# Taps in 64x64 tiles and a reordered front part, in a fused long convolution and MLP

## The chip, the cores and the metric

The kernel runs on one core of a Trainium2 chip. The metric is device time of one execution in microseconds (us). The core has five engines that run beside each other: PE (TensorE, with its weight loads, PEld), DVE (VectorE), ACT (ScalarE), POOL (GpSimd) and SP, which only issues DMAs here. Each works through its own queue in order and waits on the others by semaphores.

## The reference

Sequence length S = 2048, width D = 512, hidden width 1376, bf16 in and out. A causal convolution of four taps on k, a product with v, a convolution as long as the sequence (by FFT in the reference), a gate, and an MLP:

```
k_shift = sum over t of k_pad[:, t:t+S, :] * shift_k[:, 3-t]      # 4 taps, causal
kv      = k_shift * v
y       = irfft(rfft(kv padded to 2S) * rfft(ssm_k padded)) [:S]  # along the sequence, per channel
y       = bf16(y) + kv * ssm_D
h       = q + layernorm(q) * y
out     = h + relu(layernorm(h) @ w1) @ w2
```

## The kernel before

The long convolution is done with discrete Fourier transforms as matmuls, split in two factors. The program order within each engine is written out by hand. Its stages:

1. **Setup.** Tables of sines are made: DVE computes phases (`turns2`), ACT takes the sine (`sines2`, L146), POOL negates (`negated`, L224) into `tab`; POOL also builds `ind`, `ident`, `identw`, `f1w`, the tap weights `wdiag` (L209) and the phases of the inverse tables. `kfl` (the filter, one row per channel and 64 tokens) comes by eight DMAs on SP's and ACT's queues. k and v come transposed (channels on partitions) by eight transposing DMAs on SP's queue, alternating, into `kT` and `vT`; then `x0` (the first tokens of q) and `w1`.
2. **Filter, stage 1** (`stage1`, eight calls `s1`): row-tiled matmuls of kfl with `f1hi` and `f1lo` (L311); ACT and DVE each copy one of the two PSUM pairs into `a1k`.
3. **Taps** (`taps`, eight units `tap`): per unit, two channel blocks of eight matmuls, 128x128 diagonal weights on 512 columns of kT (L339); DVE multiplies the sum with vT in place (L342).
4. **Filter, stage 2** (`second_k`, sixteen calls): eight matmuls with `tab` (L352), copied back into a1k by ACT or DVE.
5. **Rows** (`row`, four calls of `to_rows`): PE transposes vT, two bf16 taken as one fp32 word (L289), and DVE copies the words into `xfl` (L290).
6. **Pairs** (`stage1_pairs`, eight calls): stage 1 for xfl, into `a1x` (L326).
7. **Products** (`product`, sixteen calls): stage 2 for a1x in two orders (u2, u1), each multiplied with a1k. DVE takes u2 (L493); u1 goes to POOL through an ACT copy `usb` (L492, L498) or to DVE.
8. **Inverse**: matmuls with `wd` (L518), a DVE transpose (L523), casts by ACT and POOL (`rounded`), last matmuls with `tf` (L550, L560), the gate (L587, L588).
9. **MLP**: first half L630 with relu on ACT (L666), second half L684, end sum on DVE (L690), output DMAs.

The first norm of q's first tokens (`stats`, `norm_rows`) and the centering of w1 (`column_means` on PE, `center` on POOL) lie between 4 and 6. PSUM is four pairs of banks, handed out in turn by `bank2`: two pools of two, so that each fifth request waits for the reader of the first.

Of the kernel before, what the change touches and what calls it, by code (L numbers as in the profile page):

```python
# [9 lines left out]
ALU = mybir.AluOpType  # L10
# [5 lines left out]
P = 128  # L16
# [39 lines left out]
def kernel(  # L56
# [36 lines left out]

    kfl = front.tile([P, 64, 2, 64], BF16, name="kfl")

    def load_rows(eng, rg):
        for d in range(2):
            src = bass.AP(tensor=A_ssm_k.tensor, offset=A_ssm_k.offset + S * (P * rg + 64 * d), ap=[[64, 32], [S, 64], [1, 64]])
            eng.dma_start(out=kfl[32 * rg:32 * rg + 32, :, d, :], in_=src)

    wsh = consts.tile([P, DC, KS], BF16, name="wsh")
    nc.scalar.dma_start(out=wsh[:], in_=A_shift_k.rearrange("(r p) j -> p r j", p=P))
    scratch = rows.tile([P, 4096], I32, tag="r", name="scratch")
    drow = scratch[:, 4064:4096].bitcast(BF16)
    nc.gpsimd.memset(drow, 0.0)
# [4 lines left out]
    vT = front.tile([P, DC, S], BF16, name="vT")  # L110
    CH = 512
    kT = [front.tile([P, DC, CH + 16], BF16, name=f"kT{c}") for c in range(4)]
    nc.vector.memset(kT[0][:, :, 0:16], 0.0)
    for c in range(4):
        if c == 0:
            nc.sync.dma_start_transpose(out=kT[c][:, :, 16:CH + 16], in_=k_d[0:CH, :])
        else:
            nc.sync.dma_start_transpose(out=kT[c][:], in_=k_d[CH * c - 16:CH * c + CH, :])
        nc.sync.dma_start_transpose(out=vT[:, :, CH * c:CH * c + CH], in_=v_d[CH * c:CH * c + CH, :])

    x0 = front.tile([P, 4, D], BF16, name="x0")
    for b, src in enumerate(_tokens(x_d, 0, 4)):
        nc.sync.dma_start(out=x0[32 * b:32 * b + 32].rearrange("p t d -> p (t d)"), in_=src)


    w1 = w1p.tile([P, DC, DFF], BF16, name="w1")
    for i in range(2):
        for d in range(2):
            nc.sync.dma_start(out=w1[64 * i:64 * i + 64, 2 * d:2 * d + 2],
                                in_=B_w1.rearrange("(c i d g) f -> i d g c f", c=2, i=2, d=2)[i, d])  # L130
# [29 lines left out]
    for s in range(0, P, 64):  # L160
        nc.gpsimd.iota(n2i[s:s + 64, :], pattern=[[0, 1]], base=0, channel_multiplier=1)
    r2 = scratch[:, 0:1024].rearrange("p (a b) -> p a b", b=64)
    nc.gpsimd.iota(r2, pattern=[[2, 16], [128, 64]], base=1, channel_multiplier=0)
    ident = consts.tile([P, P], BF16, name="ident")
# [3 lines left out]

    identw = consts.tile([P, P], F32, name="identw")
    nc.gpsimd.memset(identw[:], 0.0)  # L170
    nc.gpsimd.affine_select(out=identw[:], in_=identw[:], compare_op=ALU.not_equal, fill=1.0,
                            base=0, pattern=[[-1, P]], channel_multiplier=1)

    ind = consts.tile([P, P], BF16, name="ind")
    nc.gpsimd.memset(ind[:], 0.0)
    for s in range(0, P, 32):
        nc.gpsimd.affine_select(out=ind[s:s + 32, :], in_=ind[s:s + 32, :], compare_op=ALU.not_equal, fill=1.0,
                                base=0, pattern=[[-1, P]], channel_multiplier=4)

# [11 lines left out]
    load_rows(nc.scalar, 3)  # L191
    f1hi = consts.tile([P, 64], BF16, name="f1hi")
# [10 lines left out]
    nc.gpsimd.memset(f1w[:], 0.0)  # L203
    for rg in range(DC):
        for i, f in enumerate((f1hi, f1lo)):
            nc.gpsimd.tensor_copy(out=f1w[32 * rg:32 * rg + 32, i, rg % 2, :], in_=f[32 * rg:32 * rg + 32, :])
    wdiag = rows.tile([P, DC, KS, P], BF16, name="wdiag")
    for rg in range(DC):
        nc.gpsimd.tensor_tensor(out=wdiag[:, rg, :, :], in0=ident[:].unsqueeze(1).to_broadcast([P, KS, P]),  # L209
                                in1=wsh[:, rg, :].unsqueeze(2).to_broadcast([P, KS, P]), op=ALU.mult)  # L210
    wm = rows.tile([P, 4, 344], F32, name="wm")
    ones = consts.tile([P, P], BF16, name="ones")
    nc.gpsimd.memset(ones[:], 1.0 / D)

    def turns2(i, b):
        ta = scratch[:, 1024 * (b + 1):1024 * (b + 2)].rearrange("p (a b) -> p a b", b=64)
        _turns(ta, r2, n2c[:], 8192, o2[:, i, b:b + 1])
        return ta
# [7 lines left out]

    o2 = consts.tile([P, 2, 2], F32, name="o2")
    for i in range(2):
        for b in range(2):
            nc.vector.tensor_scalar(out=o2[:, i, b:b + 1], in0=n2c[:], scalar1=32.0 * i, scalar2=4096.0 + 2048.0 * b,  # L230
                                    op0=ALU.mult, op1=ALU.add)
    for b in range(2):
        sines2(0, b, turns2(0, b))
    negated(0)
    negated(1)
# [12 lines left out]
    nc.gpsimd.iota(r3[:], pattern=[[1, 64]], base=0, channel_multiplier=0)  # L248
    for i, (top, bottom) in enumerate(((64.0, 96.0), (48.0, 80.0), (32.0, 64.0), (6144.0, 8192.0))):
        nc.gpsimd.memset(ow[0:64, i:i + 1], top)  # L250
        nc.gpsimd.memset(ow[64:128, i:i + 1], bottom)
    for i in range(3):
        nc.gpsimd.tensor_scalar(out=t3[:, i, :], in0=r3[:], scalar1=n2c[:], scalar2=ow[:, i:i + 1], op0=ALU.mult, op1=ALU.add)
    nc.gpsimd.memset(hsc[:], 0.0)
    nc.gpsimd.memset(hbi[:], 0.0)
    nc.gpsimd.tensor_scalar(out=k1o[:], in0=k1c[:], scalar1=2.0, scalar2=1.0, op0=ALU.mult, op1=ALU.add)
    for b in range(4):
        q = slice(32 * b, 32 * b + 32)
        nc.gpsimd.memset(hsc[q, b % 2:b % 2 + 1], TURN / 8192)
        nc.gpsimd.memset(hbi[q, b % 2:b % 2 + 1], -0.5 * TURN)  # L260
        nc.gpsimd.tensor_scalar(out=ofc[q], in0=k1o[q], scalar1=32.0 * (b % 2), scalar2=ow[q, 3:4], op0=ALU.mult, op1=ALU.add)
    nc.gpsimd.iota(rf[:], pattern=[[1, NT], [16, 2], [64, 32]], base=0, channel_multiplier=0)
    nc.gpsimd.tensor_scalar(out=rf[:], in0=rf[:], scalar1=k1o[:], scalar2=ofc[:], op0=ALU.mult, op1=ALU.add)
# [21 lines left out]
    def to_rows(src, q, fl):  # L285
        words = src[:].bitcast(F32).rearrange("p c (a b) -> p c a b", b=32)
        pst = bank2("pst")
        for i in range(8):
            nc.tensor.transpose(out=pst[:, i // 4, P * (i % 4):P * (i % 4) + P], in_=words[:, :, :, 8 * q + i], identity=identw[:])  # L289
        nc.vector.tensor_single_scalar(out=fl[:].bitcast(I32)[:, :, :, 8 * q:8 * q + 8],  # L290
                                       in_=pst[:].bitcast(I32).rearrange("p b (i d g) -> p g d (b i)", i=4, d=2),
                                       scalar=0, op=ALU.bitwise_or)
# [4 lines left out]
    def stage1(fl, a_out, gb, engs, spike=False):  # L297
# [9 lines left out]
        for gi in range(8):  # L307
            for f, first in ((f1hi, True), (f1lo, False)):
                for rg in range(4):
                    rw = slice(32 * rg, 32 * rg + 32)  # L310
                    nc.tensor.matmul(out=outs[rg][:, gi, :], lhsT=fl[rw, 8 * gb + gi, :, :].rearrange("p d n -> p (d n)"),  # L311
                                     rhs=f[rw, :], start=first and not spike, stop=not first,
                                     tile_position=(32 * rg, 0), skip_group_check=True)
# [6 lines left out]
    def stage1_pairs(fl, a_out, gb, engs):  # L320
        pss = [bank2("ps1") for _ in range(2)]
        for gi in range(8):
            for i in range(2):
                for h in range(2):
                    rw = slice(64 * h, 64 * h + 64)
                    nc.tensor.matmul(out=pss[h][:, gi // 4, P * (gi % 4):P * (gi % 4) + P],  # L326
                                     lhsT=fl[rw, 8 * gb + gi, :, :].rearrange("p d n -> p (d n)"),
# [7 lines left out]
    def taps(c, h):  # L335
        ps = bank2("pkv")
        for i in range(2):
            for j in range(KS):
                nc.tensor.matmul(out=ps[:, i, :], lhsT=wdiag[:, 2 * h + i, j, :],  # L339
                                 rhs=kT[c][:, 2 * h + i, 16 - j:CH + 16 - j], start=(j == 0), stop=(j == KS - 1))  # L340
        vv = vT[:, 2 * h:2 * h + 2, CH * c:CH * c + CH]
        nc.vector.tensor_tensor(out=vv, in0=ps[:], in1=vv, op=ALU.mult)  # L342
# [38 lines left out]
    s1 = lambda gb: stage1(kfl, a1k, gb, "AD", spike=True)  # L381
    tap = lambda u: taps(u // 2, u % 2)
# [11 lines left out]
    qn0 = consts.tile([P, 4, D], BF16, name="qn0")  # L394
# [3 lines left out]
    def stats(src, mv, r, q):  # L398
        for i in range(4):
            nc.vector.bn_stats(out=st[:, i, :], in_=src[:, i, :])  # L400
        for i in range(4):
# [11 lines left out]
    xfl = None  # L413

    def row(q):
        nonlocal xfl
        if xfl is None:
            xfl = rows.tile([P, 64, 2, 64], BF16, tag="r", name="xfl")
        to_rows(vT, q, xfl)
# [5 lines left out]
    s1(0)  # L425
    s1(1)
    tap(0)
    s1(2)
    sines2(1, 0, turns2(1, 0))
    tap(1)  # L430
    s1(3)
    s1(4)
    tap(2)
    s1(5)
    sines2(1, 1, turns2(1, 1))
    negated(2)
    negated(3)
    tap(3)
    s1(6)
    s1(7)  # L440
    tap(4)
# [318 lines left out]
```

## Time and profile before

| | |
|---|---|
| median of 3 runs | 212.49 us (211.99 to 213.83) |
| the profiled execution | 212.53 us |
| its span | 210.8 us |
| busy in the span | PE 176.0, PEld 107.3, DVE 146.5, ACT 93.6, POOL 91.5 us |
| mean granted clock of PE | 0.984 |
| first stage-1 matmuls in a run | 14.63 us |
| last copy of the pair stage ends | 72.50 us |
| first inverse matmul that needs all products | 101.16 us |
| DMA | 16.00 MB in 47315 packets |

The span is from the first to the last instruction of the core; the rest of the execution's time lies around it. A group's line gives its line in the code, engine, operation, output and inputs with shapes, count, then busy time and mean duration in ns, then the idle time just before it and which engine's work ended that. The chain of waits is followed back from the last instruction to whatever released each piece.

### The profile page before, as it was taken

Reading aid. Unit: us, or ns where it says so; the run is one execution under the profiler, and the core shown is the slowest. Engines: PE = TensorE matmul, PEld = TensorE weight load, DVE = VectorE, ACT = ScalarE, POOL = GpSimd, SP = SyncE. Lnnn points to the kernel's source line nnn. Section 1 sums busy time; section 2 is a strip of 40 time slices with the busy share of each in tenths; the row PEclk is TensorE's granted clock in tenths of the full one; section 3 lists DMA queues with packets and bytes.
Section 4 is the critical chain, followed back from the end, with each engine's and each line's share of the span. In section 5 each row is a group of like instructions: output and inputs, shape, how many; then the busy total and the mean of one; then the engine's idle time right before and its main releaser. Section 6 shows DMA issues by size and latency. Waiting matters only on the chain.

```text
span 210.8 us, 4349 instructions
## 1 busy us (share of the span) xinstructions
PE 176.0 (84%) x1787; PEld 107.3 (51%) x1787; DVE 146.5 (69%) x236; ACT 93.6 (44%) x108; POOL 91.5 (43%) x109
## 2 busy tenths in 40 slices
PE   0329696998989587777796899999999999999993
PEld 0125343557768475665665564545455444444452
DVE  2615988459968689999998987988988381343042
ACT  0333535456288756651399447700560056016400
POOL 4899855402069569999298452031040002002000
PEclk9999997999999999999997999999999999999999
DMA  8999999920000000000780261251250215121012
GB/s 124 217 257 177 161 151 225 218 59 2 3 0 3 3 0 5 0 3 0 193 205 3 50 215 53 50 51 28 69 106 0 60 45 99 25 50 25 3 45 55
DMA packets 47315, 16.00 MB, mean 76 GB/s; under 512 B 42720, under 2 KB 46144, under 8 KB 47296
## 3 DMA queue, kind: packets, MB, share of 16 engines
q1 hardware_dynamic: 38400, 14.61, 35.5%
q10 hardware_dynamic: 8896, 1.12, 3.4%
q8 instruction: 14, 0.23, 0.5%
q14 instruction: 5, 0.04, 0.1%
HBM read 7.54 MB, written 2.10 MB: 46 GB/s over the span
## 4 chain that ended last, share of the span: by engine, by line
PE 59%; DVE 24%; ACT 4%; issue 4%; DMA 3%; ACTq 2%; POOL 1%; DVEq 0%; POOLq 0%
PE m L630 18%; PE m L684 17%; PE pkv L339 7%; DVE a1x L493 6%; DVE zs L523 5%; PE u L352 4%; DMA kfl<-in_A_ssm_k_dram 3%; DVE a1k L498 3%; PE pz L550 3%; PE ps L326 3%; PE ps2k L352 3%; DVE xfl L290 2%; ACT a1x L273 2%; PE pz L560 2%; DVE vT L342 2%
## 5 line engine op out<-in xcount | busy, mean ns | idle before, releaser
L666 ACT ACTIVATE h1T<-m 128x512 bf16<-128x512 f32 (+1 forms) x44 | 25.9, 597 | 43.6 <-PE m L630 43.6
L630 PE MATMUL m<-hT,w 128*128 128x512 bf16 (+1 forms) x176 | 39.0, 379 | 0.2 <-ACT hT L597 0.2
L684 PE MATMUL m<-w,h1T 128*128 128x512 bf16 (+1 forms) x165 | 36.3, 379 | 0.0
L690 DVE SCALAR_TENSOR_TENSOR o<-m,rstd,hp 128x256 bf16<-128x256 f32 x32 | 13.8, 478 | 27.6 <-PE m L684 26.6
L404 POOL TENSOR_SCALAR rstd<-mv 128x4 f32<-128x4 f32 x8 | 1.8, 228 | 71.2 <-DVE mv L402 71.2
L630 PEld LDWEIGHTS <-w 128*128 128x128 bf16 (+1 forms) x176 | 17.4, 100 | 20.4 <-issue 0.8
L498 POOL TENSOR_TENSOR a1k<-usb,a1k 128x1024 fp32r<-128x1024 f32 x10 | 23.7, 2396 | 5.3 <-DVE a1x L493 5.2
L684 PEld LDWEIGHTS <-h1T 128*128 128x128 bf16 (+1 forms) x165 | 15.9, 98 | 19.4 <-issue 0.3
L352 PE MATMUL u<-a1x,tab 64*128 64x256 f32 x256 | 19.8, 292 | 6.5 <-DVE a1x L493 2.4
L531 ACT CAST a1x<-zs 128x1024 fp32r<-128x1024 f32 (+2 forms) x10 | 17.2, 1717 | 11.9 <-DVE zs L523 11.9
L352 PEld LDWEIGHTS u<-a1x,tab 64*128 64x128 f32 x256 | 16.4, 185 | 9.8 <-issue 4.9
L493 DVE TENSOR_TENSOR a1x<-u,a1k 128x1024 fp32r<-128x1024 f32 x16 | 19.1, 1217 | 2.4 <-PE u L352 2.4
L529 POOL CAST a1x<-zs 128x1024 fp32r<-128x1024 f32 (+1 forms) x8 | 15.6, 1955 | 8.3 <-DVE zs L523 8.3
L523 DVE STREAM_TRANSPOSE zs<-pi 128x1024 f32<-128x1024 f32 x16 | 18.4, 1213 | 0.5 <-PE pi L518 0.5
L339 PE MATMUL pkv<-kT,wdiag 128*128 128x512 bf16 x64 | 18.5, 441 | 0.2 <-ACT a1k L273 0.2
L518 PE MATMUL pi<-a1k,wd 128*128 128x512 f32 x32 | 13.9, 434 | 2.9 <-DVE a1k L496 1.1
L342 DVE TENSOR_TENSOR vT<-pkv,vT 128x1024 bf16<-128x1024 f32 x8 | 9.8, 1221 | 9.2 <-PE pkv L339 8.2
L273 ACT CAST a1k<-ps2k 128x1024 fp32r<-128x1024 f32 x12 | 11.7, 1013 | 8.8 <-PE ps2k L352 8.8
L492 ACT COPY usb<-u 128x1024 f32<-128x1024 f32 x10 | 10.1, 1017 | 10.6 <-POOL a1k L498 8.7
L518 PE MATMUL pi<-a1x,wd 128*128 128x512 f32 x32 | 13.1, 408 | 0.0
L275 DVE CAST a1k<-ps 128x1024 fp32r<-128x1024 f32 x8 | 9.6, 1215 | 5.0 <-PE ps L311 5.0
L224 POOL TENSOR_SCALAR tab<-tab 128x1024 fp32r<-128x1024 f32 x4 | 11.0, 2775 | 4.4 <-ACT tab L146 4.3
(104 smaller groups left out, 268.3 us busy)
## 6 DMA issues: line engine op xcount, KB each, us to landing
xall<-in_A_q_dram SPq DMA_DIRECT2D x16, 128.0 KB, 3.3
out_dram<-o SPq DMA_DIRECT2D x62, 32.0 KB, 1.6
w<-in_B_w_dram SPq DMA_DIRECT2D x4, 344.0 KB, 7.3
w<-in_B_w_dram SPq DMA_DIRECT2D x1, 1280.0 KB, 6.2
kfl<-in_A_ssm_k_dram SPq DMA_DIRECT2D x4, 256.0 KB, 5.2
kfl<-in_A_ssm_k_dram ACTq DMA_DIRECT2D x4, 256.0 KB, 6.4
x<-in_A_q_dram SPq DMA_DIRECT2D x4, 128.0 KB, 3.8
hT<-hp SPq DMA_TRANSPOSE x7, 3.2
```

What stands on the lines that cost most here:

```text
L273: nc.scalar.copy(out=o, in_=i)
L339: nc.tensor.matmul(out=ps[:, i, :], lhsT=wdiag[:, 2 * h + i, j, :], rhs=kT[c][:, 2 * h + i, 16 - j:CH + 16 - j], start=(j == 0), stop=(j = ...
L352: nc.tensor.matmul(out=ps[:, d, 256 * i:256 * i + 256], lhsT=tab[rw, k1, b:b + 2, :].rearrange("p b k -> p (b k)"), rhs=a_in[rw, c, k1, :] ...
L493: nc.vector.tensor_tensor(out=spot(a1x, kp), in0=u2[:], in1=kk.bitcast(F32), op=ALU.mult)
L498: (nc.gpsimd if pool else nc.vector).tensor_tensor(out=kk, in0=(usb if pool else u1)[:], in1=kk.bitcast(F32), op=ALU.mult)
L518: nc.tensor.matmul(out=ps[:, b, :], lhsT=wd[:, m:m + 2, :].rearrange("p b k -> p (b k)"), rhs=src[:, d, 16 * b:16 * b + 16, c0:c0 + 32], s ...
L523: nc.vector.transpose(out=zs[:], in_=ps[:].rearrange("p b (k c) -> p c (b k)", c=32))
L529: nc.gpsimd.tensor_copy(out=o, in_=i)
L531: nc.scalar.copy(out=o, in_=i)
L630: nc.tensor.matmul(out=ps1[:fsz].rearrange("p (i t) -> p i t", i=4), lhsT=w1[:, c, fc * P:fc * P + fsz], rhs=hT[sc][:, c // 2, :, c % 2, : ...
L666: nc.scalar.activation(out=h1T[:fsz, fc, :], in_=ps1[:fsz], func=ACT.Relu)
L684: nc.tensor.matmul(out=ps2[:], lhsT=lhsT, rhs=w2[:ksz, fc, :], start=(fc == 0), stop=(fc == NFC - 1))
```

## The change

- `taps` runs in 64x64 tiles: the diagonal weights are 64 wide, each unit has sixteen matmuls in four tile positions, and in odd channel blocks the two halves of 64 channels change places, so that the four positions write four different halves of two banks. The sum is copied to `ksh` (bf16) by DVE or ACT and not multiplied there.
- The exchange is carried through: kfl's rows, `ind`, w1's rows, the gate and the end sum take their halves in the new order (`first_channel`, `half`). The end sum (L690 before) is three instructions per tile where it was two.
- v is loaded as rows (`vfl`), by six plain DMAs behind all k transposes; then x0 (now straight into `qn0`) and half of the v rows, then w1.
- `to_rows` transposes ksh in bf16 (sixteen per row) and multiplies with vfl straight from PSUM; `xfl` has groups of four channels innermost and lies in a pool that is opened when `early` is closed.
- All four sine blocks of `tab` come ahead of stage 1; `wdiag`, the negations, `f1w` and the inverse phases follow each other on POOL.
- The order of second_k, taps and the statistics of the first norm is new, and so are the engines of their copies.
- Products on POOL: 0, 1, 3-7, 9-12 (before 0, 1, 3, 4, 6, 7, 9, 10, 12, 13), with three `usb` buffers for two. Three matmuls `warm` on w1 follow the products.

The core of the diff:

```diff
+    def first_channel(rg, d):
+        return 128 * rg + 64 * (d ^ (rg % 2))
+    def half(t, d):
+        return t[..., 0:4:3, :] if d == 0 else t[..., 1:3, :]
...
+    vfl = front.tile([P, 64, P], BF16, name="vfl")
+    def load_v(r):
+        for d in range(2) if r % 2 else (0,):
+            n = 64 if r % 2 else P
+            src = bass.AP(tensor=A_v.tensor, offset=A_v.offset + first_channel(r, d), ap=[[64 * D, 32], [D, 64], [1, n]])
+            nc.sync.dma_start(out=vfl[32 * r:32 * r + 32, :, 64 * d:64 * d + n], in_=src)
...
-    def to_rows(src, q, fl):
-        words = src[:].bitcast(F32).rearrange("p c (a b) -> p c a b", b=32)
-        pst = bank2("pst")
-        for i in range(8):
-            nc.tensor.transpose(out=pst[:, i // 4, P * (i % 4):P * (i % 4) + P], in_=words[:, :, :, 8 * q + i], identity=identw[:])
-        nc.vector.tensor_single_scalar(out=fl[:].bitcast(I32)[:, :, :, 8 * q:8 * q + 8], in_=pst[:].bitcast(I32)..., op=ALU.bitwise_or)
+    def to_rows(q, fl):
+        toks = ksh[:].rearrange("p c (a b) -> p (c a) b", b=64)
+        pst = bank2("pst")[:].rearrange("p b n -> p (b n)").bitcast(BF16)
+        for i in range(16):
+            nc.tensor.transpose(out=pst[:, P * i:P * i + P], in_=toks[:, :, 16 * q + i], identity=ident[:])
+        for d in range(2):
+            nc.vector.tensor_tensor(out=fl[:, :, d, 16 * q:16 * q + 16].rearrange("p h i l -> p i h l"),
+                                    in0=pst.rearrange("p (i d h l) -> p i d h l", d=2, h=16, l=4)[:, :, d],
+                                    in1=vfl[:, 16 * q:16 * q + 16, 64 * d:64 * d + 64].rearrange("p i (h l) -> p i h l", l=4),
+                                    op=ALU.mult)
...
-    def taps(c, h):
+    def taps(c, a, eng):
         ps = bank2("pkv")
-        for i in range(2):
-            for j in range(KS):
-                nc.tensor.matmul(out=ps[:, i, :], lhsT=wdiag[:, 2 * h + i, j, :],
-                                 rhs=kT[c][:, 2 * h + i, 16 - j:CH + 16 - j], start=(j == 0), stop=(j == KS - 1))
-        vv = vT[:, 2 * h:2 * h + 2, CH * c:CH * c + CH]
-        nc.vector.tensor_tensor(out=vv, in0=ps[:], in1=vv, op=ALU.mult)
+        for j in range(KS):
+            for e in range(2):
+                for b in range(2):
+                    p = slice(64 * e, 64 * e + 64)
+                    d = e ^ b
+                    nc.tensor.matmul(out=ps[64 * d:64 * d + 64, b, :], lhsT=wdiag[p, 2 * a + b, j, :],
+                                     rhs=kT[c][p, 2 * a + b, 16 - j:CH + 16 - j], start=(j == 0), stop=(j == KS - 1),
+                                     tile_position=(64 * e, 64 * d), skip_group_check=True)
+        copy(eng, ksh[:, 2 * a:2 * a + 2, CH * c:CH * c + CH], ps[:])
...
+    def pairs_pool():
+        inverse_tables()
+        pl.pop("early")
+        xp = pl.push("xp", side="right")
...
+    load_k(0) ... load_k(3); load_v(0); load_v(2); load_x0(); load_v(1); load_v(3); load_w1()
+    sines2(0, 0, ta00); ta10 = turns2(1, 0); sines2(0, 1, ta01); ta11 = turns2(1, 1)
+    diagonals(); negated(0); negated(1); sines2(1, 0, ta10); sines2(1, 1, ta11)
+    negated(2); negated(3); paired(); inverse_turns()
+    s1 0 1 2, tap 0 D, s1 3 4, tap 1 A, s1 5 6, tap 2 D, s1 7, second_k 0 A, 1 D, tap 3 A, second_k 2 A, tap 4 D,
+    second_k 3 A, 4 D, tap 5 A, second_k 5 D, bn_stats, tap 6 A, second_k 6 A, bn_stats, second_k 7 D, tap 7 A,
+    bn_stats x2, moments, pairs_pool, second_k 8 A, row 0, second_k 9 A, norm_rows(0, qn0, qn0), second_k 10 A, row 1,
+    second_k 11 D, 12 A, column_means(0), row 2, second_k 13 A, 14 A, row 3, second_k 15 D, column_means(1), center 0 to 3
...
-    for kp in range(16):
-        product(kp, kp % 3 != 2 and kp < 14)
+    for kp in range(16):
+        product(kp, kp in (0, 1, 3, 4, 5, 6, 7, 9, 10, 11, 12))
+    warm(3, w1[:, 0, 0:512])
```

In the lines on the order, calls are written on one line, and D or A is the engine of a copy (DVE or ACT).

More of the change, by code (lines that the diff above doesn't have):

```diff
@@ L167 @@
                             base=0, pattern=[[-1, P]], channel_multiplier=1)
[L169 to L178, printed above, removed]
+    ones = consts.tile([P, P], BF16, name="ones")
+    nc.gpsimd.memset(ones[:], 1.0 / D)
     k1c = consts.tile([P, 1], F32, name="k1c")
@@ L191, with turns2 @@
     load_rows(nc.scalar, 3)
+    o2 = consts.tile([P, 2, 2], F32, name="o2")
+    for i in range(2):
+        for b in range(2):
+            nc.vector.tensor_scalar(out=o2[:, i, b:b + 1], in0=n2c[:], scalar1=32.0 * i, scalar2=4096.0 + 2048.0 * b,
+                                    op0=ALU.mult, op1=ALU.add)
+    def turns2(i, b):
+        ta = early.tile([P, 16, 64], I32, tag="ta", name="ta", bufs=2)[:]
+        _turns(ta, r2, n2c[:], 8192, o2[:, i, b:b + 1])
+        return ta
+    ta00 = turns2(0, 0)
+    ta01 = turns2(0, 1)
     f1hi = consts.tile([P, 64], BF16, name="f1hi")
@@ L255 @@
[L255 to L262, printed above, removed]
@@ L379, in center, with warm @@
                                 op=ALU.subtract)
-    s1 = lambda gb: stage1(kfl, a1k, gb, "AD", spike=True)
-    tap = lambda u: taps(u // 2, u % 2)
+    def warm(n, data=zero[:]):
+        ps = bank2("warm")
+        for i in range(n):
+            nc.tensor.matmul(out=ps[:, i % 2, :], lhsT=data[:, 0:P], rhs=data, start=True, stop=True)
+    s1 = lambda gb, engs: stage1(lambda g: kfl[:, g], a1k, gb, engs, spike=True)
+    tap = lambda u, eng: taps(u // 2, u % 2, eng)
     def second_ks(*kps):
@@ L417, in row @@
         if xfl is None:
-            xfl = rows.tile([P, 64, 2, 64], BF16, tag="r", name="xfl")
-        to_rows(vT, q, xfl)
+            xfl = xp.tile([P, 16, 2, 64, 4], BF16, name="xfl")
+        to_rows(q, xfl)
     def seconds(kps, engs):
@@ L423, in seconds @@
             second_k(kp, eng)
[L425 to L435, printed above, removed]
+    load_k(0)
+    load_k(1)
+    load_k(2)
+    load_k(3)
+    load_v(0)
+    load_v(2)
+    load_x0()
+    load_v(1)
+    load_v(3)
+    load_w1()
+    sines2(0, 0, ta00)
+    ta10 = turns2(1, 0)
+    sines2(0, 1, ta01)
+    ta11 = turns2(1, 1)
+    diagonals()
+    negated(0)
+    negated(1)
+    sines2(1, 0, ta10)
+    sines2(1, 1, ta11)
     negated(2)
     negated(3)
[L438 to L441, printed above, removed]
-    seconds(range(0, 2), "AA")
-    tap(5)
-    seconds(range(2, 5), "ADA")
-    tap(6)
-    seconds(range(5, 6), "A")
-    tap(7)
-    stats(x0, mv1, rstd1, 0)
-    seconds(range(6, 8), "AA")
+    paired()
+    inverse_turns()
+    s1(0, "AD")
+    s1(1, "AD")
+    s1(2, "AD")
+    tap(0, "D")
+    s1(3, "AD")
+    s1(4, "AD")
+    tap(1, "A")
+    s1(5, "AD")
+    s1(6, "AD")
+    tap(2, "D")
+    s1(7, "AD")
+    second_k(0, "A")
+    second_k(1, "D")
+    tap(3, "A")
+    second_k(2, "A")
+    tap(4, "D")
+    second_k(3, "A")
+    second_k(4, "D")
+    tap(5, "A")
+    second_k(5, "D")
+    nc.vector.bn_stats(out=st[:, 0, :], in_=qn0[:, 0, :])
+    tap(6, "A")
+    second_k(6, "A")
+    nc.vector.bn_stats(out=st[:, 1, :], in_=qn0[:, 1, :])
+    second_k(7, "D")
+    tap(7, "A")
+    nc.vector.bn_stats(out=st[:, 2, :], in_=qn0[:, 2, :])
+    nc.vector.bn_stats(out=st[:, 3, :], in_=qn0[:, 3, :])
+    moments(mv1, rstd1, 0)
+    pairs_pool()
+    second_k(8, "A")
     row(0)
+    second_k(9, "A")
+    norm_rows(0, qn0, qn0)
+    second_k(10, "A")
     row(1)
-    seconds(range(8, 10), "AA")
-    norm_rows(0, qn0, x0)
+    second_k(11, "D")
+    second_k(12, "A")
+    column_means(0)
     row(2)
+    second_k(13, "A")
+    second_k(14, "A")
     row(3)
-    inverse_tables()
-    pl.pop("early")
-    seconds(range(10, 13), "ADA")
-    column_means(0)
-    seconds(range(13, 14), "D")
+    second_k(15, "D")
     column_means(1)
-    for n in range(4):
+    for n in (0, 1):
         center(n)
-    seconds(range(14, 16), "AD")
+    for n in (2, 3):
+        center(n)
     pl.pop("front")
@@ L468 @@
     for gb in range(8):
-        stage1_pairs(xfl, a1x, gb, "AA" if gb == 4 else "AD")
-    pl.pop("rows")
+        stage1_pairs(lambda g: xfl[:, g // 4, :, :, g % 4], a1x, gb, ("DA", "AD", "AD", "AD", "AA", "AD", "AD", "AD")[gb])
+    pl.pop("xp", "rows")
     late = pl.push("late")
@@ L577, in gate_both, with gate @@
                                             in_=hp[q][:, d].rearrange("p i c -> p (i c)"))
-    def gate(q, d, pool, half=None):
+    def gate(q, d, pool, part=None):
         if d == 0:
```

183 lines of the change are left out of this document (101 added, 82 removed).

## The prediction

> **What bounds the kernel now.** I read the busy table by stretches first, then the chain of waits, the queue of each engine in time order, and the groups by shape for prices. The stretches (columns: bounds, length, busy time with instruction count of PE, PEld, DVE, ACT, POOL, granted clock, DMA share, GB/s):
>
> ```profile
> 14.60:16.70 2.10, 2.07 (x129) 1.96 (x130) 0.99 (x1) 1.01 (x1) 2.02 (x4) 1.00 1.16 230
> ...
> 32.00:34.60 2.60, 1.27 (x99) 1.06 (x100) 2.60 (x3) 2.04 (x3) 0.81 (x1) 0.98 1.29 271
> 34.60:38.10 3.50, 3.45 (x10) 1.01 (x9) 1.31 (x2) 0.96 (x2) 3.50 (x2) 0.52 0.67 159
> ...
> 62.00:73.00 11.00, 8.23 (x244) 7.05 (x238) 9.19 (x8) 9.07 (x10) 9.20 (x4) 1.00 0.01 3
> 73.00:101.00 28.00, 21.18 (x260) 17.03 (x260) 25.45 (x23) 13.29 (x13) 23.75 (x10) 1.00 0.00 1
> ```
>
> Nothing multiplies before 14.6, when the last kfl rows land. From there to 72.5, when the last a1x copy of the pair stage ends, the change rewrites nearly everything; behind that it touches only the products (73 to 101) and small things. The chain of waits (start, length, what) shows who sets the pace:
>
> ```profile
> 16.73 3.58 PE pkv L339 x8
> ...
> 34.65 3.49 PE pkv L339 x8
> 38.14 1.15 PE ps2k L352 x16
> 39.29 1.84 PE pkv L339 x8
> ...
> 72.50 0.62 issue
> ...
> 101.03 0.14 issue
> ```
>
> The taps (L339) are 14.5 us of this chain: eight matmuls take 1.84, and 3.5 where the clock is half (0.52 granted after a stretch in which PE was busy 1.27 of 2.6). DVE carries the rest: s1 copies, tap products (L342), table turns, later rows (L290). Prices, by shape:
>
> ```profile
> L498 POOL TENSOR_TENSOR a1k<-usb,a1k 128x1024 fp32r<-128x1024 f32 x10 | 23.7, 2396 | 5.3 <-DVE a1x L493 5.2
> ...
> L342 DVE TENSOR_TENSOR vT<-pkv,vT 128x1024 bf16<-128x1024 f32 x8 | 9.8, 1221 | 9.2 <-PE pkv L339 8.2 <-DMA w<-in_B_w_dram 1.0
> ...
> L588 DVE TENSOR_TENSOR hp<-hp,xall 128x1024 bf16<-128x1024 bf16 x3 | 2.1, 691 | 0.1
> ...
> L596 PE MATMUL m<-ident,hp 128*128 128x128 bf16 x8 | 0.8, 222 | 0.0
> ```
>
> DVE copies start 1.13 to 1.14 apart in a run, ACT copies 0.95 (duration 1.01). I carried each engine's queue forward with such spacings, each of the four PSUM pairs waiting for its reader. For the old order this ends the pair stage at 72.5, as the trace does. I do the same with the new order.
>
> **The change, part by part.** *Taps.* 64 matmuls of 128x512 become 128 of 64x64 weights and 512 columns, four to a step, four steps to a tap. No row has 64x64 tiles. If four overlap as the row-tiled ones do (L352: eight in 0.56 warm, four steps of two with 256 columns, 0.03 above streaming half of L630's 0.216), a step is 0.25 and a tap 1.0; bounds 0.9 and, one matmul at a time, 16 x 0.213 = 3.4. I take 1.0, and 2.0 for the first at half clock.
>
> *14.6 to 28.5.* The second half of the table leaves this stretch: four DVE turn instructions (1.42 a pair) and two sines move into DVE's and ACT's idle time before 15.7. DVE idled 4.55 there and ACT 3.32, and the turns' operand r2 no longer waits 2.18 for drow's landing. The DVE queue is then ten copies (eight s1, taps 0 and 2): 15.7 + 10 x 1.13 + 1.4 of waits for the cold first PE work = 28.4. Before, the last s1 copy ended at 35.9.
>
> *28.5 to 40.8.* PE: eight second_k of 0.56 and five taps of 1.0 = 9.5, so 38.0; tap 7's copy ends at 39.1, and row(0)'s sixteen bf16 transposes (L596: eight in 0.65) at 40.6. DVE has four copies, the first norm's statistics (2.4 + 0.3), and the two masks of inverse_tables (0.8): 40.8.
>
> *An added wait.* xfl now lies where the early pool was, and POOL's wd reads w3 from that pool. POOL can write wd only behind rstd (0.23 + 1.04 after the moments at 40.0) and its own 0.70: 42.1. So row(0)'s product starts 1.3 late; the four norm_rows, row(1) and second_k(11)'s copy stand behind it on DVE, and PE waits for their PSUM pairs.
>
> *Rows from PSUM.* One 1.21 instruction per row becomes two bf16 products of 1024 elements; the eight tap products (9.8) disappear, replaced by three DVE and five ACT copies. No row shows bf16 PSUM operands. Bounds: L588's 0.69 (all bf16) and L342's 1.22 (fp32 from PSUM). In this trace the two-operand DVE rows of 1.2 have a 4-byte operand and the all-bf16 ones take 0.69, so I take 0.69 (0.64 apart). DVE from 42.1: four products, norm 1.3, a copy 1.13 = 47.2; PE delivers row(2) at 47.5 and row(3) at 49.9 behind second_k and column means; the last product ends at 51.3.
>
> The Trainium skill (VectorE: DVE Perf Modes, § The perf-mode tier table) lists tensor_tensor with any PSUM operand at the unpacked rate, while its next section on PSUM operands still allows packed 16-bit pairs. By the table the row would be 1.22 and the sum that of the first rival.
>
> *Pairs.* Weights are read at a stride of four; the old transposes read theirs at a stride of 128 bytes with 0.193 per fp32 load beside 0.185 for contiguous L352, so I price it at nothing (if a load grew past the copies that cover it, 0.3 per group, 2.4). First pair at 51.7, and 10.9 as before (61.63 to 72.50): 62.6, against 72.50: -9.9. The walk leaves PE idle 1.8 before second_k(0); the like idling at 32 to 34.6 was followed by a half-clock stretch that cost 1.7. I charge half: **-9.1**, with 0.9 either way.
>
> *DMA.* SP loses four v transposes (2.95 + 3.11 + 3.72 + 3.16 = 12.9 of its queue) and gains six row loads: eight 256 KB units at kfl's 1.43 (5.72 for four) = 11.4. k moves ahead of v; x0 and w1 stay behind. w1 landed by 44; column_means needs it at 44.7. Priced at nothing; if a unit took ACT's 2.31, w1 would come 5.5 late and most of that would show. The rest of POOL's moved setup (f1w 3.7, inverse turns 7.7) stands behind the four negations, which end near 23.5, so near 35, before its readers at 40; five us later it would show directly.
>
> *Products.* POOL takes 11 of them for 10, DVE 21 operations for 22. Before, POOL ran from 75.79 to 100.26 with little idle, and DVE's last needed piece ended at 101.03; pi started at 101.16, 28.66 behind the pair stage. Now POOL: 3.29 + 11 x 2.40 = 29.7 plus 0.1. DVE's saving is hidden behind POOL, and the third usb buffer only keeps POOL fed: **+1.2** (0.8 at its fastest, 2.374). PE then idles about 3, but for warm's three matmuls; pi at half clock is spaced 0.43 in place of 0.24 (the trace has that at 115.0): **+0.3**, 0 to 1.2.
>
> *Behind that.* The permuted halves keep every element count. L690 goes from 32 instructions to 48 (one of 0.48 split in two per tile): about 0.25 x 16 = 4 on DVE, which has 51 of 88 busy there while the chain is PE throughout; priced at nothing, 1.0 if the four tiles of one block lose their cover. The swapped kfl and w1 rows, ind, and the missing identw cost nothing, being off every wait shown.
>
> **Sum.** -9.1 + 1.2 + 0.3 = -7.6: a span of 203.2 for 210.8. The profiled execution took 212.53, so 1.7 lie around the span: 205.0. Its time equals the median of 212.49 within 0.04.
>
> **Rivals.** *Rows at the unpacked rate (25%).* Eight products of 1.22 add 4.3 to DVE; 1.3 of it fills its waits for row(2) and row(3): +3.0, 208.0. For it: no bf16 PSUM row exists. Against it: L588.
>
> *Tiles overlap only in twos (11%).* Each tap keeps 1.85, all eight on PE's path: 205.0 + 8 x 0.85 = 211.8, about no change. For it: L311, L326 and L352 all write another bank for each row tile, while the new taps send two row tiles into one bank.
>
> The Trainium skill (TensorEngine Tiling (Array Packing), § Gotcha 1: PSUM Pressure) says that different row tiles cannot access one bank at the same time; no run here shows it yet, and here the two write different partitions of the bank. By that rule this rival's time holds.
>
> *Tiles don't overlap at all (11%, slower).* Sixteen matmuls of 0.213 one behind another: 3.4 a tap, 205.0 + 8 x 2.4 = 224.2. Between these the line is straight: above 1.94 us a tap the change loses, above 2.2 by more than 1%. For it: narrow weight loads have no cheap row (96 columns 0.123, 128 columns 0.098). Against it: L352's pairs overlap with fp32 loads of 0.185.
>
> *v or w1 late (5%).* column_means waits for w1: half of the 5.5 above gives 208. Against it: the DMA share falls to 0.04 at 44.
>
> **How the numbers follow.** The forecast has 48%, from 202.5 to 207. About 1% is what this kernel's runs can tell from no change (211.99 to 213.83). Faster by more: the forecast, rows, DMA and 2% of the twos = 80%; within: the other 9%; slower: 11%. The range runs from 201.5 (all low bounds, no half clock) to 210.5, which leaves the twos and the serial case out.
>
> **What would show it.** Right: eight tap groups of about 1.0; last s1 copy near 28.5; row(0)'s first product released by POOL's wd near 42; row products of 0.7; first pair near 52; POOL without idle time through the products, pi released by POOL; the MLP lines as long as before. Wrong: tap groups of 1.8 or more; 1.2 row products; PE waiting for DMA in column_means; a granted clock near 0.5 in a second stretch; products that end with DVE.

## The result and the profile after

The changed kernel takes 211.22 us (median of 20 runs, 209.94 to 212.72) where the kernel before takes 212.30 in the same comparison: a ratio of 0.994, 95% interval 0.991 to 0.997. It is faster by half a per cent, less than the 1% that the prediction named as the least it could tell from no change, and 6.2 us slower than the 205.0 forecast. The profiled execution took 212.38 with a span of 210.6 (before 210.8). It is one of the slower of the twenty, 1.2 above their median, so the stretches below account for its span and not for the median's.

The changed kernel's stretches (bounds, length, busy time with instruction count of PE, PEld, DVE, ACT, POOL, granted clock, DMA share, GB/s):

```profile
14.60:34.72 20.12, 13.77 (x585) 9.53 (x585) 12.28 (x11) 10.05 (x10) 17.39 (x42) 1.00 0.98 177
...
23.73:26.62 2.89, 0.01 (x2) 0.00 (x1) 0.34 (x1) 0.09 (x1) 2.55 (x14) 1.00 1.23 241
...
34.86:38.50 3.64, 3.64 (x32) 2.34 (x32) 1.23 (x1) 1.02 (x1) 0.00 (x0) 0.53 0.83 131
60.65:71.50 10.85, 8.66 (x257) 7.76 (x256) 8.43 (x8) 9.55 (x10) 5.78 (x3) 1.00 0.01 3
71.50:100.80 29.30, 21.36 (x262) 17.18 (x263) 25.41 (x23) 14.11 (x15) 25.84 (x11) 1.00 0.01 1
```

The first row is the stretch that the prediction ends at 28.4: it ends at 34.72. In it PE works 13.8 of 20.1 us, DVE 12.3 and ACT 10.1: no engine is full. The second row lies inside it: 2.89 us in which PE does nothing, and DVE and ACT next to nothing. The third is a stretch at half clock. The pair stage (fourth) is as long as foretold, but starts at 60.65 and not at 51.7.

Its chain of waits (start, length, what), from two windows of it:

```profile
18.33 1.88 PE pkv L375 x16
20.23 1.24 DVE ksh L305
...
23.73 2.88 issue
...
26.91 1.85 PE pkv L375 x16
...
34.86 2.08 PE ps2k L388 x16
36.94 1.67 PE pkv L375 x16
38.61 0.67 PE ps2k L388 x8
39.28 0.99 PE pkv L375 x16
```
```profile
96.09 4.67 POOL a1k L581 x2
100.77 0.04 issue
100.81 0.76 PE pi L610 x2
```

A tap at full clock now takes 0.99 (1.84 before), and the products end with POOL. But 2.88 us of the chain are "issue": PE waits for nothing that the profile shows. PE's own timeline shows where (start, length, and in brackets the idle time before and its releaser):

```profile
21.52 0.40 PE L336 MATMUL ps<-drow,ind 32*128 32x256 bf16 x4 [1.33 <-DVE ksh L305]
26.62 0.24 PE L343 MATMUL ps<-f1hi,kfl 32*128 32x64 bf16 x4 [2.88 <-issue]
```

The second idle time is in the middle of a unit: 4 + 64 matmuls of s1(3) and 4 + 56 of s1(4) have run since 21.52, 128 in all, and the last eight stand still. With its weight load each makes 256 PE instructions between the ends of the two idle times. The page's list of DMA queues, and the same list for 24.0 to 25.1 alone (packets, MB, share of 16 engines), name what comes in such pieces:

```profile
q8 instruction: 15, 0.25, 0.5%
```
```profile
q8 instruction: 1, 0.02, 5.9%
```

Fifteen packets of 16 KB for PE's 1881 matmuls and 1886 weight loads: one for each 251. One lies in 24.0 to 25.1 (0.059 x 16 engines x 1.1 = 1.04 us of one engine), and PE resumes 1.5 us after it; another, narrowed in the same way, lies between 19.3 and 20.3, and PE resumes at 21.52. From 21.52 to 26.62, 5.10 us, PE got exactly one block and worked 2.22.

Groups by shape, for the prediction's prices:

```profile
L581 POOL TENSOR_TENSOR a1k<-usb,a1k 128x1024 fp32r<-128x1024 f32 x11 | 25.8, 2384 | 7.7 <-DVE a1x L576 7.7
...
L783 DVE SCALAR_TENSOR_TENSOR o<-m,rstd,hp 128x128 bf16<-128x128 f32 x32 | 9.7, 346 | 25.0 <-PE m L777 24.8 <-PE m L779 0.2
...
L358 PEld LDWEIGHTS <-xfl 64*128 64x128 bf16 x256 | 7.8, 111 | 2.2 <-issue 1.8
...
L319 PEld LDWEIGHTS <-ksh 128*128 128x128 bf16 x64 | 6.1, 202 | 1.0 <-ACT ksh L303 0.7
L321 DVE TENSOR_TENSOR xfl<-pst,vfl 128x1024 bf16<-128x1024 bf16 x8 | 5.3, 705 | 3.8 <-POOL wd L299 2.1 <-PE pst L319 1.7
```

### The profile page after: what moved, and what is told of

The parts are those of the page before. It is cut to its first block, busy times and chain, and to the rows that moved or that the text cites. A ratio compares the mean times of both kernels' runs of the same rounds, so it can differ in the third digit from the quotient of the medians.

```text
span 210.6 us, 4557 instructions
## 1 busy us (share of the span) xinstructions
PE 173.0 (82%) x1881; PEld 109.7 (52%) x1886; DVE 145.9 (69%) x254; ACT 98.0 (47%) x112; POOL 92.4 (44%) x109
## 4 chain that ended last, share of the span: by engine, by line
PE 57%; DVE 21%; issue 7%; POOL 5%; ACT 4%; ACTq 3%; POOLq 0%; DVEq 0%
PE m L722 18%; PE m L777 17%; DVE zs L615 5%; DVE a1x L576 5%; PE pkv L375 4%; POOL a1k L581 3%; PE ps2k L388 3%; PE u L388 3%; DVE a1k L305 3%; PE pz L642 3%; PE ps L358 3%; ACTq L107 3%; ACT a1x L303 2%; PE pz L652 2%; PE ps L343 2%
## 5 line engine op out<-in xcount | busy, mean ns | idle before, releaser
L448 POOL TENSOR_SCALAR rstd<-mv 128x4 f32<-128x4 f32 x8 | 2.4, 295 | 74.5 <-DVE mv L446 74.5
L783 DVE SCALAR_TENSOR_TENSOR o<-m,rstd,hp 128x128 bf16<-128x128 f32 (+1 forms) x48 | 15.8, 389 | 25.6 <-PE m L777 24.8
L581 POOL TENSOR_TENSOR a1k<-usb,a1k 128x1024 fp32r<-128x1024 f32 x11 | 25.8, 2384 | 7.7 <-DVE a1x L576 7.7
L777 PEld LDWEIGHTS <-h1T 128*128 128x128 bf16 (+1 forms) x165 | 16.0, 98 | 19.3 <-issue 0.3
L615 DVE STREAM_TRANSPOSE zs<-pi 128x1024 f32<-128x1024 f32 x16 | 18.5, 1217 | 1.2 <-PE pi L610 1.2
L343 PE MATMUL ps<-f1hi,kfl 32*128 32x64 bf16 x256 | 8.7, 232 | 10.8 <-DMA kfl<-in_A_ssm_k_dram 6.6
L575 ACT COPY usb<-u 128x1024 f32<-128x1024 f32 x11 | 11.0, 1015 | 9.2 <-PE u L388 6.0
L343 PEld LDWEIGHTS <-kfl 32*128 32x128 bf16 x512 | 8.2, 122 | 11.7 <-issue 6.3
L414 POOL TENSOR_TENSOR w<-w,wm 128x1376 bf16<-128x1376 bf16 x4 | 11.3, 2852 | 5.0 <-ACT wm L410 5.0
L388 PE MATMUL ps2k<-a1k,tab 64*128 64x256 f32 x128 | 11.1, 311 | 2.2 <-DVE a1k L305 2.2
```

Source lines behind the costliest of these rows:

```text
L343: nc.tensor.matmul(out=outs[rg][:, gi, :], lhsT=data(8 * gb + gi)[rw].rearrange("p d n -> p (d n)"), rhs=f[rw, :], start=first and not spi ...
L388: nc.tensor.matmul(out=ps[:, d, 256 * i:256 * i + 256], lhsT=tab[rw, k1, b:b + 2, :].rearrange("p b k -> p (b k)"), rhs=a_in[rw, c, k1, :] ...
L581: (nc.gpsimd if pool else nc.vector).tensor_tensor(out=kk, in0=(usb if pool else u1)[:], in1=kk.bitcast(F32), op=ALU.mult)
L615: nc.vector.transpose(out=zs[:], in_=ps[:].rearrange("p b (k c) -> p c (b k)", c=32))
L777: nc.tensor.matmul(out=ps2[:], lhsT=lhsT, rhs=w2[:ksz, fc, :], start=(fc == 0), stop=(fc == NFC - 1))
L783: nc.vector.scalar_tensor_tensor(out=of(o[:], d)[:, a], in0=ps[:, a], scalar=rstd2[:, t, :], in1=pair(hp[sc][:, d, i, :])[:, a], op0=ALU.m ...
```

## The experiments

The theory: between 14.6 and the last s1 copy PE has 1170 instructions, 4.6 blocks of 256, and blocks come too slowly. The forecast of 13.9 us for them would need one every 3.0 us. Rivals: PE waits for copies or PSUM there; the half clock is the cause and not the effect; the transfers are to blame. All ratios below are to the kernel before on the same chip. There its median is 212.85 to 213.38, while the expectations reckon from 211.2 for the changed kernel (212.3 before), so ratios are the safer comparison.

**Half as many s1 instructions (e1_pairs).** s1 goes through the pair stage's function: 64 rows a matmul, against the block-diagonal table f1w, which DVE now builds:

```diff
-    s1 = lambda gb, engs: stage1(lambda g: kfl[:, g], a1k, gb, engs, spike=True)
+    s1 = lambda gb, engs: stage1_pairs(lambda g: kfl[:, g], a1k, gb, engs, spike=True)
+                    # spike: for b, h in (0,0) (0,1) (1,0) (1,1), 64 rows each
+                    nc.tensor.matmul(out=pss[h][:, b, :]...[:, :, :, 0:32], lhsT=ind[rw, :], rhs=dpair[rw, :, ...],
+                                     start=True, stop=False, tile_position=(64 * h, 0), skip_group_check=True)
```

> The changed kernel with s1 done in 64-row pairs, as the pair stage does it: 72 PE instructions (weight loads included) per s1 unit for 136, the same sums; DVE builds the weights f1w itself. Theory (PE's instruction supply: PE's instructions arrive in blocks of 256, and a block takes 4 to 5 us to come, so PE stands still at 20.2 for 1.33 and at 23.7 for 2.88): with 704 instead of 1216 instructions between 14.6 and the last s1 copy both standstills vanish, the last s1 copy ends at 28.5 to 31 instead of 34.7, and the time is 204 to 206.5 (4.5 to 7 below 211.2). Rival (PE waits there for copies or for PSUM, or the half clock is the cause and not the effect): PE's streaming per unit grows from 1.0 to about 1.3, the standstills stay or move, the last s1 copy ends at 34 to 36, and the time is 211 to 213.

Measured: 207.42 (206.73 to 208.21), ratio 0.975 (0.970 to 0.980), span 206.3. PE's waits from 14 to 36 (what waited for what, total, times, longest):

```profile
PE ps L343 <- DMA kfl<-in_A_ssm_k_dram: 3.5, 1, 3.5
PE ps2k L373 <- DVE a1k L304: 1.4, 1, 1.4
```

Both standstills are gone. s1 started 1.2 us later than in the changed kernel (15.76; its rows landed later), so the last s1 copy ended at 32.2, not by 31; the stretch from s1's start to that end is 16.5 instead of 20.1, although a unit's matmuls stream longer (1.09 to 1.14 at full clock for 0.68). The time is 0.9 above the theory's range; the rival's 211 to 213 is well off. Of the 4.0 us by which the first pair is earlier (56.62 for 60.65), 2.5 are gained by the last s1 copy and 1.5 behind it, where second_k and tap(3) no longer fell to half clock (1.22 for 2.08, 0.99 for 1.67).

**The same instructions without the transfers (e2_noload).**

```diff
-    load_k(1); load_k(2); load_k(3); load_v(0); load_v(2); load_x0(); load_v(1); load_v(3); load_w1()
+    for c in (1, 2, 3):
+        kT[c] = kT[0]
...
     s1(7, "AD")
+    nc.vector.memset(qn0[0:32], 0.0)
+    load_x0()
+    load_w1()
```

> The changed kernel without most transfers between 11 and 30: three quarters of k and all of v are not loaded (the taps read the first quarter, the rows are multiplied by kfl), and x0 and w1 are issued behind s1(7). PE's instructions are the same as in the changed kernel. Theory a (the supply of instructions is slow because the transfers fill the DMA engines): both standstills of PE shrink to 0.5 or less, the last s1 copy ends at 28.5 to 30, time 204.5 to 206.5. Theory b (a block of 256 instructions takes about 4 us to come even through idle DMA engines): standstills of 0.5 to 1.5 stay at the same two places of the program, the last s1 copy ends at 31 to 33, time 207 to 209.5. Theory c (the supply has nothing to do with it): standstills as before, 1.33 and 2.88, time within 1 of 211.2.

Measured: 207.56, ratio 0.978 (0.972 to 0.983), span 206.0, last s1 copy 30.46. PE's timeline and two stretches:

```profile
19.70 0.29 PE L328 MATMUL ps<-drow,ind 32*128 32x256 bf16 x4
...
23.00 0.21 PE L335 MATMUL ps<-f1hi,kfl 32*128 32x64 bf16 x4 [1.19 <-issue]
```
```profile
21.81:23.00 1.19, 0.00 (x1) 0.00 (x0) 0.37 (x1) 0.00 (x0) 1.19 (x1) 1.00 0.00 0
25.86:26.45 0.59, 0.00 (x1) 0.00 (x0) 0.58 (x1) 0.35 (x1) 0.47 (x4) 1.00 0.05 14
```

Theory b is the nearest, at its low edge: with the DMA engines at a share of 0.00 and 0.05 PE still stands for 1.19 and 0.59, and the ends are one block and 26.45 - 23.00 = 3.45 us apart. The last s1 copy lies between the ranges of a and b, and the places are not quite those foretold: the standstill ahead of s1(3) is gone, the one in s1(4) stays where it was, and the next comes one block later. So a block has a time of its own, and it is longer among the transfers (5.10). The first line settles a detail: the profile puts the idle time at 20.18 in the changed kernel down to the ksh copy, but here s1(3) starts at 19.70, while that copy runs to 21.05. In the program s1(3) waits for the readers of its two PSUM pairs only, which had ended by 19.7 in the changed kernel. I count that 1.33 to the supply as well. Its end also lies 0.05 behind the copy's, so this trace alone leaves it open; that it ends exactly one block ahead of the second standstill, and behind a packet like the others (the count in all traces, below), speaks for the supply.

**The count put back (f1_more).** e1_pairs with 32 more matmuls a unit:

```diff
+                    if spike:
+                        nc.tensor.matmul(out=pss[h][:, gi // 4, P * (gi % 4):P * (gi % 4) + 8], lhsT=zero[rw, 0:P],
+                                         rhs=zero[rw, 0:8], start=False, stop=False, ...)
```

> The kernel of e1_pairs with 32 matmuls more in each s1 unit that add zero (8 columns each, zero weights), so that a unit again has 136 PE instructions where e1_pairs has 72. If PE's instruction supply is what stands still (3.5 us a block of 256 with idle DMA engines in e2_noload, about 5 with busy ones): standstills of PE of 2 to 5 us together come back between 18 and 28, the last s1 copy ends at 34 to 36 instead of 32.2, time 210 to 213. If the count does not matter and e1_pairs was faster for its 64-row tiles: time within 1 of e1_pairs' 207.4.

Measured: 211.81, ratio 0.992 (0.987 to 0.996). PE's waits:

```profile
PE ps L348 <- issue: 2.2, 1, 2.2
```

A standstill comes back, at the low edge of what was expected: 2.17 of the 4.3 us by which the first pair is later than in e1_pairs (60.88, 56.62). Much of the rest is streaming, since at full clock a unit's matmuls take 1.45 to 1.53 for 1.09 to 1.14. So about half of it belongs to the count. The last s1 copy ended at 36.5, 0.5 behind the expected range.

**A warm start (g2_warm).** The changed kernel with throw-away matmuls ahead of s1:

```diff
+    warm(47, wz[:])
     s1(0, "AD")
```

> The changed kernel (s1 in its four 32-row tiles, 136 PE instructions a unit) with 47 throw-away matmuls of 256 columns ahead of s1, so that it starts at the full clock. If the half clock is what makes the stretch long: the last s1 copy ends 2 to 3 sooner than 34.7 and the time is 208 to 209. If the instruction supply sets the pace: PE only reaches its standstills sooner and stands longer (5 to 7 us together instead of 4.2), last s1 copy 33 to 34.7, time 210.2 to 211.5.

Measured: 215.11, ratio 1.007 (1.003 to 1.012), profiled span 211.7. Waits of PE, one stretch and two lines of PE's timeline:

```profile
PE ps L345 <- issue: 6.2, 3, 3.0
```
```profile
17.96:20.94 2.98, 0.00 (x1) 0.00 (x0) 0.55 (x1) 0.32 (x1) 2.98 (x2) 0.70 1.24 115
```
```profile
20.94 0.24 PE L345 MATMUL ps<-f1hi,kfl 32*128 32x64 bf16 x2 [2.98 <-issue]
21.48 1.92 PE L377 MATMUL pkv<-kT,wdiag 64*64 64x512 bf16 x16
```

The half clock is the effect here: PE starts at full clock, runs sooner into the end of a block, stands 2.98, the grant falls in that stretch, and tap 0 takes 1.92 again. The standstills add up to 6.2, as the supply theory had it; that the kernel became slower by over 1% (1.007 for 0.994) neither theory expected. In the profiled execution, the fastest of the ten, s1 starts 0.8 later than in the changed kernel (15.31), and the last s1 copy (35.63) and the first pair (61.55) are 0.9 later: the warm start bought nothing, and the late start shows. Why the other executions take longer still (213.5 to 217.3) stays open.

**The same in e1_pairs (f3_warm).** 36 such matmuls, with f1w as data.

> The kernel of e1_pairs with 36 throw-away matmuls of 256 columns ahead of s1 (in PE's idle time before 15), so that s1 starts at the full clock. If the half clock at the start is on the path (the first two units took 1.86 and 1.71 instead of 1.30): 0.6 to 1.6 faster than e1_pairs, 205.8 to 206.8, last s1 copy about 31. If the last sine (ACT to 16.7) and the copies set the pace there: within 0.5 of 207.4.

Measured: 206.15, ratio 0.969 (0.963 to 0.975). Where instructions suffice, the warm start is worth about 1.3 us: the interval overlaps that of e1_pairs, but the first pair is 1.65 earlier (54.97 for 56.62).

**The kernel before with pairs alone (g3_before_pairs).** The same `s1` line as in e1_pairs.

> The kernel before with one part of e1_pairs alone: its s1 in 64-row pairs (72 PE instructions a unit for 136). If e1_pairs was faster because fewer instructions have to be supplied: nothing to gain here, where 4.5 blocks had 21 us and PE stood still for 0.48 and 0.27 only: 0 to 0.8 faster, or up to 1 slower for the longer streaming (1.06 for 0.9 a unit), 211.5 to 213.5. If pairs are better in themselves (copies, clock): 3 to 5 faster, as in the changed kernel.

Measured: 212.09, ratio 0.994 (0.991 to 0.998): 1.3 us, more than the 0.8 expected, where the same step gave the changed kernel 4 (0.994 to 0.975). But the profile shows none of it in the stretch that was edited: the first pair starts at 61.61, for 61.47 in the kernel before. The span is 0.7 shorter for a stretch far behind it: from 113 to 123 the granted clock is 1.00 where the kernel before has 0.83. So in that profile pairs gained nothing by themselves ahead of the pair stage; why the grant differs there stays open.

**The kernel before with the sines first (e4_sines).**

```diff
     for b in range(2):
         sines2(0, b, turns2(0, b))
+    for b in range(2):
+        sines2(1, b, turns2(1, b))
```

> The kernel before with one part of the change alone: the second half of the table's turns and sines moved ahead of s1. By the step of the prediction (DVE's queue sets the pace of that stretch) four turn instructions of together 3.1 us leave it: 2 to 3 us faster, 209.3 to 210.3. By the theory of instruction supply PE already had 1152 instructions (4.5 blocks of 256) between 14.6 and 35.9, 4.7 us a block, and its two small standstills (0.48 and 0.27) grow to 1 to 3 us together: 0 to 1 us faster, 211.3 to 212.3.

Measured: 210.23, ratio 0.990 (0.982 to 0.998): nearer the prediction's size than the supply theory's, though the interval reaches into both. The two stretches, to the last s1 copy and from there to the first pair, in e4_sines and in the kernel before:

```profile
14.94:35.35 20.41, 17.25 (x571) 10.07 (x577) 15.21 (x13) 9.04 (x9) 19.36 (x38) 1.00 1.15 194
35.35:59.08 23.73, 22.12 (x201) 15.58 (x201) 17.69 (x25) 12.62 (x15) 4.28 (x5) 1.00 0.31 69
```
```profile
14.60:35.90 21.30, 17.66 (x573) 10.01 (x574) 16.84 (x16) 10.11 (x10) 15.97 (x36) 0.97 1.19 188
35.90:61.47 25.57, 24.01 (x206) 16.15 (x205) 17.70 (x26) 12.61 (x15) 6.80 (x6) 0.96 0.28 62
```

Of 3.1 us of DVE work taken out, the stretch itself gave 0.9; 1.8 came behind it, where PE no longer fell to half clock. I expected the first and had not thought of the second. At 4.5 us a block (20.41 for 4.5 blocks) the old order is near what the supply bears, and its standstills are 0.62 and less.

**wd early (e3_wd).** The changed kernel with `inverse_tables()` called behind tap(3).

> The changed kernel with inverse_tables called behind tap(3) instead of behind the moments, so that POOL writes wd near 40 and the first row product no longer waits for it (2.06 of DVE idle at 48.9). Theory (the added wait sits on the chain): row(0)'s first product starts at 49.0 instead of 50.9, the first pair at 58.7 to 59.7 instead of 60.65, time 209.2 to 210.2. Rival (DVE's lost 2 us are filled again while it waits for row(2) and row(3)): first pair within 0.5 of 60.65, time within 0.5 of 211.2.

Measured: 211.38, ratio 0.992 (0.988 to 0.996), no different from the changed kernel's 0.994. POOL's wd is done at 39.1 and nothing waits for it, but from row(0)'s transposes to the first pair it is 12.9 us for 13.3 (45.61 to 58.54, 47.32 to 60.65). DVE's lost 2.06 was filled again while it waited for row(2) and row(3): its row products wait 3.9 for PE's transposes, where the changed kernel has 1.7 and the wait for wd. The rival is right. This profile's first pair is early for another reason: second_k(0) and (1) ran at full clock (1.21 for 2.08).

**The old taps in e1_pairs (f2_t128).** Eight matmuls of 128x512 a tap:

```diff
-            for e in range(2):
-                for b in range(2):
-                    nc.tensor.matmul(out=ps[64 * d:64 * d + 64, b, :], lhsT=wdiag[p, 2 * a + b, j, :], ...)
+        for b in range(2):
+            for j in range(KS):
+                nc.tensor.matmul(out=ps[:, b, :], lhsT=wdiag[:, 2 * a + b, j, :], ...)
```

> The kernel of e1_pairs with the taps as eight matmuls of 128x512 again (the odd blocks' diagonals with their halves swapped; the sums are the same). By the prediction's step (1.84 for 1.0 a tap, all eight on PE's path): 6.8 slower than e1_pairs, 214. Rival: the taps ahead of the last s1 copy are covered by the copies, five others stand on PE's path: 4.2 slower, 211.6. Second rival: copies set the pace everywhere: within 1 of 207.4.

Measured: 217.63, ratio 1.021 (1.016 to 1.026): 10 us slower than e1_pairs, more than any expectation. s1 started 3.9 us later (19.70) in the profile, since its rows landed late; from s1's start to row(0)'s transposes it is 33.9 against 27.5. So the taps are worth 6.4 us where PE has its instructions, nearly the 6.8 of the prediction's step, and the rest is the start.

**Candidates (f4_best, g1_best2).** f4_best is e1_pairs with f3_warm's matmuls, tap(3) ahead of second_k(0), wd early and the old sharing of the products; g1_best2 builds f1w on POOL.

> A candidate better than both kernels: e1_pairs with f3_warm's matmuls, tap(3) ahead of second_k(0) (PE idled 1.41 there), inverse_tables ahead of the moments as in e3_wd, and the products shared out as in the kernel before. Sum: warm -0.6 to -1.6, tap order -1, wd -0.4, products -0.65: 203.5 to 205, first pair near 53.5 (56.6 in e1_pairs). If the parts hide behind one another: 205 to 207.

> f4_best with the weights f1w built on POOL ahead of wdiag instead of by eight small DVE instructions (in e1_pairs to f4_best s1 started at 15.4 to 16.2, in the changed kernel at 14.5; the load issues on ACT's queue lasted longer beside these DVE instructions). If they are what held the loads up: s1 starts at 14.6 to 15.0, 0.9 to 1.5 faster than f4_best, 203.2 to 203.8. If the start varies by itself: within 0.5 of 204.7.

Measured: f4_best 204.71, ratio 0.961 (0.956 to 0.965), first pair at 53.80. g1_best2 204.23 (203.64 to 204.49), ratio 0.957 (0.953 to 0.961), where the changed kernel has 0.994: faster than both. g1_best2's gain over f4_best is the rival's size, and the intervals overlap. s1 started at 15.44, for 16.24 in f4_best, still later than the 14.6 to 15.0 foretold, so DVE's small instructions explain at most a part of the late start.

**The count in all traces.** Number PE's matmuls and weight loads from the start of the program. The standstills of these runs end at number 449 and 705 in the changed kernel and in e3_wd, at 705 and 961 in e2_noload, at 449, 961 and 1217 in g2_warm, at 705 in f1_more, and at 707 and 963 in the kernel before. They are 256 or a multiple of it apart, whatever work stands there (a few records can be missing from a trace). Each ends 1.3 to 1.7 us behind an instruction packet. This leaves no room for a copy or a PSUM bank as the cause of these.

## Why the prediction was wrong, step by step

*14.6 to 28.5* is the step that failed. It let each engine's queue run as fast as its instructions allow and gave PE all its instructions at once. The last s1 copy came at 34.72 instead of 28.4, 6.3 late. In the step's own terms, its "1.4 of waits for the cold first PE work" were 7.2 of DVE idle between the ten copies (0.43, 0.61, 1.39, 2.91 and 1.82), and the copies took 12.1 for 11.3. Behind these waits stand PE's standstills of 1.33 and 2.88 (4.2); tap 1 at half clock (1.85 for 0.99: 0.9; the rows print a grant of 1.00 there, the durations say otherwise: the 64 matmuls of a unit without a standstill take 1.03 to 1.18 up to 31, and 0.68 behind); and 0.44 in which PE waited for an ACT copy behind the last sine, which ended at 16.1 because a turn took 1.52, while POOL's negation ran, where others take 0.81. In numbers that the profile of before held: 1147 PE instructions in 21.3 us were 4.8 us a block, and the step asked for 3.0.

The kernel before showed it faintly, in two idle times of PE that the prediction read over:

```profile
26.61 0.20 PE L311 MATMUL ps<-f1hi,kfl 32*128 32x64 bf16 x3 [0.48 <-issue]
...
31.98 0.20 PE L311 MATMUL ps<-f1hi,kfl 32*128 32x64 bf16 x3 [0.27 <-issue]
```

Between their ends lie 256 PE instructions and 5.37 us: one block, at a DMA share of 1.20. PE worked 5.11 of it, so the old order fell short by little.

*The half-clock charge* was the right fear at half its size: 0.9 charged, and 34.86 to 38.5 cost (2.08 - 1.21) + (1.67 - 0.99) = 1.6.

*Rows from PSUM, 28.5 to 40.8:* the product takes 705 ns, as taken (0.69). The transposes in it were priced from contiguous loads; with ksh read at a stride of 128 bytes a weight load takes 202 ns, and a row 1.58 to 1.66 for 1.3: 1.2 in four rows. *An added wait* came as told (2.06 of DVE idle, released by POOL's wd), but e3_wd shows it nearly free; the walk had charged it.

From there all is close. Pair stage 10.85 for 10.9 (its strided loads 111 ns, no matter). Products: 71.53 (the end of ACT's last copy, as the 72.50 of before; DVE's last ends 0.4 later in both) to 100.81 is 29.28 for 28.66 before, +0.6 where +1.2 was foretold, POOL last as said. From pi on 109.8 for 109.6: +0.15 for +0.3. The split end sum (L783: 15.8 busy for 13.8 before) stayed hidden. So the sum misses by 8.15 at the first pair (60.65 for 52.5), of which the three sizes above make 6.3 + 0.7 + 1.2, and gets 0.75 back behind it: 203.2 + 7.4 = 210.6. The 1.2 takes all of the longer transposes to be on the path, which no run tried alone.

*Taps:* right, with f2_t128 behind it. The rivals on tiles fell: 0.99 a tap is four at a time, two row tiles into one bank among them. The Trainium skill (TensorEngine Tiling (Array Packing), § Gotcha 1: PSUM Pressure) holds that different row tiles cannot access one bank at the same time; here, on different partitions of the bank, they did. The first rival fell with 705 ns, and with it the rate that the skill (VectorE: DVE Perf Modes, § The perf-mode tier table) lists for tensor_tensor with a PSUM operand.

What I missed was a rival of its own: that the supply of instructions becomes the bound. The Trainium skill (Runtime: NRT & Kernel Launch, § Instruction fetch mechanics) says that each engine fetches its instructions in blocks of 256 through a DMA queue of its own while it executes, and calls the cost mostly hidden. The runs agree with the blocks; that the cost is hidden holds here for matmuls that take long (the MLP's first half, 176 of 379 ns, has 0.2 of PE idle), and not for a stretch that uses a block in 2.2 us.

## What to carry to other kernels

Count PE's instructions, weight loads included, over each stretch that you mean to shorten, and divide by 256: here a block took 3.45 us with idle DMA engines and up to 5.4 with busy ones, and a new order that asked for one every 3.0 did not get it. Small matmuls are the ones that ran short here, and fewer and wider ones (64 rows for 32) can be the better bargain though they stream longer. An "issue" idle time of PE in the middle of a group of like matmuls, however small, can be a sign that the stretch is near that bound; two of them 256 instructions apart make it likely. "Issue" pieces elsewhere in the chain (72.50 and 101.03 in the kernel before) are not of this kind.

## What the runs showed that I had not expected

- The block time is not one number: 5.10 in the changed kernel (DMA share about 1.1), 5.37 in the kernel before (1.20), 3.45 in e2_noload (0.05 and less), and yet also 3.45 once in g2_warm (33.87 - 30.42, share 0.98). The packet itself takes 0.9 to 1.4 in all of these traces. What differs most in these blocks is how long after PE's entry into one the next packet starts: 1.1 in e2_noload and 1.2 in g2_warm, 2.5 in the changed kernel, 2.8 in the kernel before. The DMA share alone does not decide it; what else does stays open.
- The start of s1 varied by 5 us between kernels that issue the same first loads (14.5 to 19.7). In f2_t128 two load issues on ACT's queue lasted 3.80 and 4.49 where e1_pairs has 2.40 and 2.53; POOL wrote a wdiag of twice the size meanwhile. Whether that is the cause was not tried.
